# Block 0 of a two-layer kernel: second-layer steps placed between first-layer chunks, w_in and w_out rounded in turn

## Chip, cores, metric

The kernel runs on one core of one Trainium2 chip. The metric is device microseconds (us) of one execution, lower is better. PE is the matmul engine, with PEld its weight loads; DVE, ACT and POOL are the vector, scalar and GpSimd engines; SP only issues DMAs here. Each engine takes its instructions in order.

## What is computed

```python
w   = softmax(weight, axis=-1)               # 8 heads, 7 taps
y   = causal depthwise convolution of x      # x: (8, 4096, 192) float32
h   = y.reshape(32768, 192) @ w_in           # w_in: (192, 2048)
g   = h * clip(h + 3, 0, 6) / 6
out = g @ w_out                              # w_out: (2048, 192)
```

`w_in` and `w_out` arrive as 64-bit floats. The kernel rounds them to 32 bits itself, from their bits, once, while it works on its first tokens.

## The kernel before

The 32768 tokens are cut into 32 blocks of 1024, and a block into two groups of 512. In each block seven taps of convolution make y. **The first layer** makes g in 16 units. A unit holds one of 8 chunks c of d_ff for one group (128 columns of the lower half of d_ff, and 128 of the upper half for the other token group); unit n has c = n mod 8. It is 18 matmuls (three passes over high and low parts of weights and y, three thirds of the 192 channels, two row halves; `products`, L439) into the two PSUM banks of one of four slots. Then ACT takes the bounded part (`relu`, L302), DVE multiplies (`gate`, L306) and the slot is free again. Units 0 to 7 read y as the convolution leaves it (`y_own`). Units 8 to 15 read `y_other`, in which the two halves of the partitions are exchanged: SP issues these swaps as DMAs (L290, L291).

**The second layer** of blocks 1 to 31 is a recursive scheme with fewer products (`second_layer`, L535). Block 0 does it directly: 12 parts (2 token groups by 6 sets of 32 output columns), four to a bank, three banks; a bank sums 64 matmuls over 16 chunks of d_ff (`mm`, L317; one such matmul is two records in the trace). A bank is then transposed by DVE (L373) and stored by SP in four DMAs (L348).

**Rounding** works on units of its own, eight for `w_in` and eight for `w_out`, each 384 KB of 64-bit words. `load` is the DMA (L143 for w_in in two halves, L151 for w_out); `split` is two DVE instructions (L181, L185); `clamp` three on ACT (L193, L196, L199); `join` two on DVE (L202, L206) and one on POOL (L210). For w_in, `part` follows: L218 on ACT, L219 and L220 on POOL. The units are kept in the list `units` (L241): first all of w_in, then all of w_out. Four are loaded at the start, and each `join` loads the unit four further on. w_out's stages have four buffers.

**Block 0's order is written out by hand** (`tc.manual_schedule`). A part of the convolution is done by PE with diagonal weights (L739): all seven taps of the last third of the channels and taps 3 to 6 of third 1. First-layer work of units 0, 1 and 8 begins by thirds, as the thirds of y come (`thirds_of`, L759), in the order: units 0 thirds 2 and 0; unit 1 thirds 2 and 0; unit 0 third 1; unit 8 thirds 2 and 0; unit 1 third 1; unit 8 third 1. Then a loop (L813) takes the units in the order 0, 1, 8, 9, 2, 10, 3, 11 and so on; in every second step one rounding unit goes on (`join` in one step, `part`, `clamp` and `split` in the next). So w_in is rounded in the loop, and most of w_out after it. Then `out_direct` (L353) does the second layer bank by bank, and within a bank chunk by chunk. Its banks are in the first three free slots. On the other engines it is interleaved with `prepare` (block 1's seven taps, L845 on ACT and six of L847 on DVE, the high part on ACT, the low part L425 on DVE, and the load of block 2's x by POOL) and with `begin_block_two` (three sums of w_out on DVE, L237, sums on POOL, L507, and block 2's first three taps). Block 1's first layer follows on PE. Its first unit takes the first free slot.

Of the kernel before, what the change touches and what calls it, by code (L numbers as in the profile page):

```python
# [20 lines left out]
HIGH, LOW, FULL = range(3)  # L21
# [10 lines left out]
def kernel(  # L32
# [8 lines left out]
    nc = tc.nc  # L41
# [8 lines left out]
    G = 2  # L50
# [10 lines left out]
    NP = NC // 2  # L61
    DH = D // 2
    QS = 32
    NQ = DH // QS
# [97 lines left out]
    class Rounding:  # L162
# [10 lines left out]
        def load(self):  # L173
            self.st = self.load_words()

        def split(self, engine=nc.vector):
            high = self.st[:, :, 1]
            self.top = cnv.tile([P, WS], U32, name="top")
            self.scale = cnv.tile([P, WS], U32, name="scale")
            self.sig = cnv.tile([P, WS], F32, name="sig")  # L180
            engine.tensor_scalar(  # L181
                out=self.scale[:], in0=high, scalar1=0x7FF00000, scalar2=None,
                op0=ALU.bitwise_and,
            )
            engine.tensor_scalar(  # L185
                out=self.top[:], in0=high, scalar1=0xFFFFF, scalar2=0x100000,
                op0=ALU.bitwise_and, op1=ALU.bitwise_or,
            )
# [12 lines left out]
        def join(self):  # L201
            nc.vector.scalar_tensor_tensor(  # L202
                out=self.scale[:], in0=self.st[:, :, 1], scalar=0x80000000,
                in1=self.scale[:], op0=ALU.bitwise_and, op1=ALU.bitwise_or,
            )
            nc.vector.scalar_tensor_tensor(  # L206
                out=self.sig[:], in0=self.top[:], scalar=2.0**-20, in1=self.sig[:],
                op0=ALU.mult, op1=ALU.add,
            )
            nc.gpsimd.tensor_tensor(  # L210
                out=self.sig[:] if len(self.dst) > 1 else self.dst[0],
                in0=self.sig[:], in1=self.scale[:].bitcast(F32), op=ALU.mult,
            )
# [13 lines left out]
    def w_in_unit(j):  # L227
        dst = [w[:, j].rearrange("p s f -> p (s f)") for w in w_in_parts]
        return Rounding(lambda: load_w_in(j), dst)

    def w_out_unit(j):
        dst = w_out[:, j, B11 : B22 + 1].rearrange("p b d -> p (b d)")
        return Rounding(lambda: load_w_out(j), [dst])
# [4 lines left out]
                out=w_out[:, :, o], in0=w_out[:, :, x], in1=w_out[:, :, y], op=ALU.subtract  # L238
            )

    units = [w_in_unit(j) for j in range(NP)] + [w_out_unit(j) for j in range(NP)]  # L241
    AHEAD = 4
    for n in range(AHEAD):
        units[n].load()
# [59 lines left out]
    def gate(g_, h):  # L304

        nc.vector.scalar_tensor_tensor(  # L306
            out=g_, in0=g_, scalar=1.0, in1=h, op0=ALU.min, op1=ALU.mult
        )

    def dff_half(k):  # L310
        return g[:, :, k // G, k % G]

    def mm(bank, j, x, w, q, ps_, first, last, tokens=slice(0, N)):

        cols = slice(q * QS, (q + 1) * QS)
        return [
            lambda p=p: nc.tensor.matmul(  # L317
                out=bank[j * QS : (j + 1) * QS, tokens], lhsT=w_out[:, p, w, cols],
                rhs=x[:, p, tokens],
                start=(first and p == ps_[0]), stop=(last and p == ps_[-1]),  # L320
                tile_position=(0, j * QS),
            )
            for p in ps_
        ]

    def side_by_side(*streams):
        for mms in zip(*streams):
            for m in mms:
                m()

    every = range(NP)

# [6 lines left out]
    def next_xt():  # L339
        xts.append(xts.pop(0))  # L340
        return results[0][:, xts[-1]]
# [3 lines left out]
    def store_rows(i, k, q, xt, j, dma=nc.sync, tokens=slice(0, N)):  # L345

        t0 = i * TB + k * N
        dma.dma_start(  # L348
            out=out[t0 + tokens.start : t0 + tokens.stop, q * QS : (q + 1) * QS].rearrange("(t r) d -> r t d", r=QS),
            in_=xt[j * QS : (j + 1) * QS, tokens].rearrange("r (t d) -> r t d", d=QS),  # L350
        )

    def out_direct(i, work):  # L353

        parts = [(k, q) for k in range(G) for q in range(G * NQ)]
        for r in range(0, len(parts), 4):
            b = 2 * free_slots[r // 4]
            bank = psum[:, b]
            streams = []
            for j, (k, q) in enumerate(parts[r : r + 4]):  # L360
                streams.append([
                    m
                    for mms in zip(*(
                        mm(bank, j, dff_half(h * G + k), h * 2 + q // NQ, q % NQ, every,
                           h == 0, h == 1)
                        for h in range(2)
                    ))
                    for m in mms
                ])
            side_by_side(*streams)  # L370
            work[r // 4]()
            xt = next_xt()
            nc.vector.transpose(out=xt[:], in_=bank)  # L373
            for j, (k, q) in enumerate(parts[r : r + 4]):
                store_rows(i, k, q, xt, j)

    def g_sums(engine, which, slots, width):

# [42 lines left out]
    def high_of(out, x):  # L421
        nc.scalar.mul(r32(out), x, CUT)
# [6 lines left out]
    def swap_parts(thirds=slice(0, K3)):  # L429
        for n in range(2):  # L430
            swap(y_other[:, n, thirds], y_own[n][:, thirds])

    def products(n, slot, s, steps=range(3), begin=False, end=False):
        group, c = divmod(n, NP)
        for m_ in steps:
            wn, yn = PASSES[m_]
            for k in range(2):
                r = slice(k * D2, (k + 1) * D2)
                nc.tensor.matmul(  # L439
                    out=psum[:, 2 * slot + k], lhsT=r32(w_in_parts[wn][r, c, s]),  # L440
                    rhs=r32(y_other[r, yn, s] if group else y_own[yn][r, s]),
                    start=begin and m_ == 0, stop=end and m_ == 2, skip_group_check=True,
                )
# [269 lines left out]
        if n < len(units):  # L713
            units[n].load()

    def join(n, more=True):
        units[n].join()
        if more:
            load(n + AHEAD)

    def part(n):
        units[n].part()
# [1 line left out]
    with tc.manual_schedule():  # L724
# [7 lines left out]

        thirds = [slice(s, s + 1) for s in range(K3)]
        pe_third = K3 - 1
        pe_taps = 3
        x0 = x_tiles[0]

        def pe_tap(b, part, k, first):
# [20 lines left out]
        def thirds_of(n, which, end=False):  # L759
            if n not in early:  # L760
                early[n] = free_slots.pop(0)
            for s in which:
                products(n, early[n], s, begin=s == pe_third, end=end)

        def high_y(s, of):
            high_of(y_own[HIGH][:, thirds[s]], of)

        def low_y(s, of):
            low_of(y_own[LOW][:, thirds[s]], of, y_own[HIGH][:, thirds[s]], nc.vector)
            swap_parts(thirds[s])  # L770

        def all_of(s):
            return y[:, thirds[s]]
# [6 lines left out]
        clamp(0)  # L780
        for u in conv0[5 : per - 3]:
            u()
        join(0, more=False)
        split(1)
        high_y(pe_third, psum[:, b : b + 1])
        part(0)
        clamp(1)
        for u in conv0[per - 3 : per]:
            u()
        low_y(pe_third, psum[:, b : b + 1])  # L790
        high_y(0, all_of(0))
        low_y(0, all_of(0))
        load(AHEAD)
        thirds_of(0, (pe_third, 0))
        join(1)
        split(2)
        for u in conv0[per + 2 : per + 2 * pe_taps]:
            u()
        part(1)
        add(y[:, 1], psum[:, b1], y[:, 1])  # L800
        high_y(1, all_of(1))
        low_y(1, all_of(1))
        clamp(2)
        split(3)
        thirds_of(1, (pe_third, 0))
        thirds_of(0, (1,), True)
        thirds_of(NP, (pe_third, 0))
        thirds_of(1, (1,), True)
        thirds_of(NP, (1,), True)

        n = 2
        for at, k in enumerate([0, 1, NP, NP + 1] + [
            c + group * NP for c in range(2, NP) for group in range(2)  # L813
        ]):
            if at == 6:
                x_tiles[1] = load_x(1)
            if k in early:
                slot = early[k]
            else:
                slot = free_slots.pop(0)  # L820
                for m_ in range(3):
                    for s in range(K3):
                        products(k, slot, s, (m_,), s == 0, s == K3 - 1)
            to, both = places(k, slot)
            relu(to, both)
            if at % 2:
                part(n)
                clamp(n + 1)
            else:
                join(n)  # L830
            gate(to, both)
            free_slots.append(slot)
            if at % 2:
                split(n + 2)
                n += 1
        while n < len(units):
            join(n)
            clamp(n + 1)
            split(n + 2)
            n += 1  # L840
        start_pools.close()

        def conv_jobs(i):
# [32 lines left out]
            for job in conv[:3]:  # L876
                job()

        out_direct(0, [prepare, lambda: None, begin_block_two])
        swap_parts()  # L880
        w_sums(((T3, B22, B12),))
        last = ctx.enter_context(tc.tile_pool(name="last", bufs=1, reuse_waits="tile"))
# [52 lines left out]
```

## Time and profile before

| | |
|---|---|
| time of three runs | 2231.13, 2230.18, 2228.7 us; median 2230.18 |
| the profiled execution | 2230.25 us; span 2228.5 us |
| PE busy | 2212.9 us, 99% of the span |
| DVE, ACT, POOL busy | 81%, 42%, 37% |
| mean granted PE clock | 0.998 |
| first matmul of block 1's first layer | 104.61 us |
| PE idle in block 0's second layer, all for POOL's rounding of w_out | 6.3 us in 5 waits |

All times within the execution are counted from the start of its span. In a table by stretches of time, each engine has its busy us and, in brackets, its instructions; the columns behind POOL are the granted PE clock (1 is full), the mean busy share of the DMA engines, and GB/s. In a list by time, a row has its start, its length, engine, line, operation, output from input, shape, count, and in square brackets the idle time before it and what ended that. Instructions of one engine overlap a little, so a row may begin before the row above it has ended.

### The profile page before, as it was taken

What the parts mean: (1) busy time and instruction counts of PE and PEld (TensorE: products, weight loads), DVE (VectorE), ACT (ScalarE), POOL (GpSimd) and SP (SyncE); (2) the same over time, 40 slices, a digit from 0 to 9 for tenths busy, and PEclk for the clock granted to TensorE, in tenths of its full rate; (3) what the DMA queues carried; (4) which work ended last, traced back from release to release, by engine and by line L of the source; (5) the groups of instructions that cost most, each with busy time, mean ns of one, the idle gap of its engine ahead of it and who ended that gap; (6) DMA issues with size and microseconds to landing.
All of it is one profiled execution on the core that took longest, in us unless ns stands there. A gap on an engine that the chain in (4) does not pass through costs nothing.

```text
span 2228.5 us, 49336 instructions
## 1 busy us (share of the span) xinstructions
PE 2212.9 (99%) x21596; PEld 1537.8 (69%) x21596; DVE 1811.0 (81%) x1590; ACT 935.1 (42%) x1172; POOL 832.5 (37%) x706
## 2 busy tenths in 40 slices
PE   9899999999999999999999999999999999999999
PEld 6377776677766777666777667776677776677766
DVE  8778888888888888888888888788888888788866
ACT  7344433344433444334444334443344433344433
POOL 4344422344322444224443234442244422344322
PEclk9999999999999999999999999999999999999999
DMA  6233223332233332333322333323333223332232
GB/s 149 59 84 77 34 58 77 70 70 51 43 75 73 66 71 37 61 77 67 73 44 48 77 70 70 63 39 68 77 63 77 36 57 77 70 70 54 41 60 34
DMA packets 249095, 142.91 MB, mean 64 GB/s; under 512 B 207120, under 2 KB 212240, under 8 KB 248880
## 3 DMA queue, kind: packets, MB, share of 16 engines
q1 hardware_dynamic: 230392, 105.86, 23.5%
q0 software_dynamic: 17248, 33.64, 8.7%
q8 instruction: 169, 2.77, 0.5%
q10 hardware_dynamic: 1240, 0.27, 0.1%
q14 instruction: 46, 0.38, 0.1%
HBM read 31.72 MB, written 25.17 MB: 26 GB/s over the span
## 4 chain that ended last, share of the span: by engine, by line
PE 97%; ACT 1%; DVE 1%; POOL 0%; issue 0%; DMA 0%; DVEq 0%; ACTq 0%; SPq 0%; POOLq 0%
PE psum L535 49%; PE psum L439 46%; PE psum L317 1%; ACT g L302 1%; PE psum L739 0%; POOL w_out L210 0%; PE psum L747 0%; ACT scale L196 0%; DVE g L306 0%; ACT sig L199 0%; ACT sig L193 0%; DMA stage<-in_moe_w_out_dram 0%; ACT w_in L218 0%; DVE scale L202 0%; DVE sig L206 0%
## 5 line engine op out<-in xcount | busy, mean ns | idle before, releaser
L535 PE MATMUL psum<-g,w_out 128*32 128x512 f32 (+1 forms) x6712 | 967.4, 552 | 0.0
L302 ACT ACTIVATE g<-psum,half 128x1024 f32<-128x1024 f32 x512 | 571.6, 1118 | 495.4 <-PE psum L439 467.3
L306 DVE SCALAR_TENSOR_TENSOR g<-g,psum 128x1024 f32<-128x1024 f32 x512 | 618.3, 1218 | 198.1 <-ACT g L302 197.8
L498 POOL TENSOR_TENSOR s<-g 128x256 f32<-128x256 f32 x248 | 268.5, 1083 | 1251.0 <-DVE g L306 914.5
L535 PEld LDWEIGHTS psum<-g,w_out 128*32 128x32 f32 x6712 | 370.8, 110 | 246.9 <-issue 126.9
L439 PE MATMUL psum<-y,w_in 64*128 64x512 f32 x4608 | 535.8, 389 | 2.5 <-ACT w_in L218 1.8
L439 PE MATMUL psum<-y_other,w_in 64*128 64x512 f32 x4608 | 529.8, 387 | 0.0
L439 PEld LDWEIGHTS psum<-y,w_in 64*128 64x128 f32 x4608 | 430.1, 185 | 120.3 <-issue 26.0
L439 PEld LDWEIGHTS psum<-y_other,w_in 64*128 64x128 f32 x4608 | 432.7, 184 | 90.7
L535 PE MATMUL psum<-s,w_out 128*32 128x512 f32 (+1 forms) x3272 | 465.4, 570 | 0.0
L847 DVE SCALAR_TENSOR_TENSOR y<-x,c_sb,y 128x1536 f32<-128x1536 f32 x186 | 335.7, 1805 | 1.2
L387 POOL TENSOR_TENSOR s<-g 128x1024 f32<-128x1024 f32 x93 | 297.7, 3201 | 25.1 <-DVE g L306 25.1
L535 PE MATMUL psum<-g,w_s 128*32 128x256 f32 x1240 | 282.8, 379 | 0.0
L535 PEld LDWEIGHTS psum<-s,w_out 128*32 128x32 f32 x3272 | 153.7, 110 | 80.1 <-issue 48.4
L535 PEld LDWEIGHTS psum<-g,w_s 128*32 128x32 f32 x1240 | 136.4, 110 | 68.3
L387 DVE TENSOR_TENSOR s<-g 128x2048 f32<-128x2048 f32 (+1 forms) x93 | 177.1, 1931 | 1.1
L535 PE MATMUL psum<-s,w_s 128*32 128x256 f32 x744 | 170.7, 379 | 0.0
L498 DVE TENSOR_TENSOR g<-g 128x1024 f32<-128x1024 f32 x124 | 151.7, 1223 | 5.3
L387 DVE TENSOR_TENSOR g<-g 128x2048 f32<-128x2048 f32 x62 | 139.0, 2283 | 0.0
L407 DVE TENSOR_TENSOR p<-psum,p 32x256 f32<-32x256 f32 (+1 forms) x93 | 47.8, 514 | 96.3 <-PE psum L535 94.8
L407 DVE TENSOR_TENSOR results<-psum,results 32x256 f32<-32x256 f32 (+3 forms) x128 | 69.3, 541 | 51.2 <-issue 47.6
L532 ACT COPY psum<-psum 32x512 f32<-32x512 f32 x93 | 51.3, 551 | 135.4 <-PE psum L535 135.4
(88 smaller groups left out, 1094.2 us busy)
## 6 DMA issues: line engine op xcount, KB each, us to landing
y_other<-y SPq DMA_DIRECT2D x124, 384.0 KB, 5.0
g<-g POOLq DMA_DIRECT2D x62, 512.0 KB, 5.0
out_dram<-results SPq DMA_DIRECT2D x378, 64.0 KB, 2.0
x<-in_x_dram SPq DMA_DIRECT2D x53, 388.5 KB, 7.1
g<-in_moe_w_in_dram SPq DMA_DIRECT2D x16, 192.0 KB, 5.1
stage<-in_moe_w_out_dram SPq DMA_DIRECT2D x8, 384.0 KB, 7.8
x<-in_x_dram SPq DMA_DIRECT2D x7, 384.0 KB, 6.4
y_other<-y SPq DMA_DIRECT2D x12, 128.0 KB, 2.3
```

The lines of the kernel that those rows point to most:

```text
L302: nc.scalar.activation(r6, h, ACT.Relu, bias=half[:], scale=1.0 / 6.0)
L306: nc.vector.scalar_tensor_tensor(out=g_, in0=g_, scalar=1.0, in1=h, op0=ALU.min, op1=ALU.mult)
L317: lambda p=p: nc.tensor.matmul(out=bank[j * QS : (j + 1) * QS, tokens], lhsT=w_out[:, p, w, cols], rhs=x[:, p, tokens], start=(first and p ...
L387: engine.tensor_tensor(out=o[:, r], in0=a[:, r], in1=b[:, r], op=op)
L407: nc.vector.tensor_tensor(out=out, in0=x, in1=y, op=op)
L439: nc.tensor.matmul(out=psum[:, 2 * slot + k], lhsT=r32(w_in_parts[wn][r, c, s]), rhs=r32(y_other[r, yn, s] if group else y_own[yn][r, s]), ...
L498: engine.tensor_tensor(out=o, in0=p, in1=q, op=op)
L532: streams[3].append((t - 0.5, lambda: fn(*args, **kw)))
L535: nc.tensor.matmul(out=out, lhsT=w, rhs=x, start=start, stop=True, tile_position=(0, j * QS), skip_group_check=True,)
L847: jobs.append(lambda k=k: nc.vector.scalar_tensor_tensor(out=y[:], in0=x[:, :, k : k + N], scalar=c_sb[:, k : k + 1], in1=y[:], op0=ALU.mu ...
```

## The change

It concerns block 0 alone.

1. `units` alternates: w_in 0, w_in 1, then w_in 2, w_out 0, w_in 3, w_out 1, and so on to w_in 7, w_out 5; then w_out 6 and 7.
2. PE does one tap more of third 1 (2 to 6), DVE one less. The swaps are issued for each part as it is ready, the high one ahead of the low one. Rounding unit 1 is split after the low parts of thirds 2 and 0 and no longer ahead of them.
3. Loads 4 to 7 are issued together after the swaps of thirds 2 and 0, ahead of those of third 1; loads 8, 9, 10 and 12 after third 1's swaps; loads 11, 13, 14 and 15 in the loop.
4. The early units are 0 and 8: both thirds 2 and 0, then both third 1. Unit 1 is no longer early.
5. The loop takes the units by chunk: 0, 8, 1, 9, 2, 10, ... A rounding unit is joined in every step from the third on.
6. The slot of the third unit is not given back after its gate: its two banks hold the second layer's first two banks. After the sixth, eighth, ... sixteenth unit PE does 16 matmuls of the second layer, those of one chunk for these two banks (`direct_chunk`).
7. After the loop: `prepare`, chunks 6 and 7 of the two banks, their transposes and stores, the slot given back; then all eight chunks of the third bank, in the first free slot; `begin_block_two`; the third bank's transpose and stores.

```diff
-    units = [w_in_unit(j) for j in range(NP)] + [w_out_unit(j) for j in range(NP)]
+    units = [w_in_unit(0), w_in_unit(1)]
+    for j in range(2, NP):
+        units += [w_in_unit(j), w_out_unit(j - 2)]
+    units += [w_out_unit(j) for j in range(NP - 2, NP)]
...
-    def out_direct(i, work):
...
+    direct = [(k, q) for k in range(G) for q in range(G * NQ)]
+    direct = [direct[r : r + 4] for r in range(0, len(direct), 4)]
+
+    def direct_chunk(banks, p):
+
+        for h in range(2):
+            for r, bank in banks:
+                for j, (k, q) in enumerate(direct[r]):
+                    for m in mm(bank, j, dff_half(h * G + k), h * 2 + q // NQ, q % NQ,
+                                every[p : p + 1], h == 0 and p == 0, h == 1 and p == NP - 1):
+                        m()
+
+    def direct_out(i, r, bank):
+        xt = next_xt()
+        nc.vector.transpose(out=xt[:], in_=bank)
+        for j, (k, q) in enumerate(direct[r]):
+            store_rows(i, k, q, xt, j)
...
-        pe_taps = 3
+        pe_taps = 2
...
         def high_y(s, of):
             high_of(y_own[HIGH][:, thirds[s]], of)
+            swap(y_other[:, HIGH, thirds[s]], y_own[HIGH][:, thirds[s]])
 
         def low_y(s, of):
             low_of(y_own[LOW][:, thirds[s]], of, y_own[HIGH][:, thirds[s]], nc.vector)
-            swap_parts(thirds[s])
+            swap(y_other[:, LOW, thirds[s]], y_own[LOW][:, thirds[s]])
...
-        join(0, more=False)
-        split(1)
+        join(0)
         high_y(pe_third, psum[:, b : b + 1])
         part(0)
-        clamp(1)
         for u in conv0[per - 3 : per]:
             u()
         low_y(pe_third, psum[:, b : b + 1])
         high_y(0, all_of(0))
         low_y(0, all_of(0))
-        load(AHEAD)
+        for n in range(AHEAD, 2 * AHEAD):
+            load(n)
         thirds_of(0, (pe_third, 0))
-        join(1)
-        split(2)
+        thirds_of(NP, (pe_third, 0))
+        split(1)
+        clamp(1)
         for u in conv0[per + 2 : per + 2 * pe_taps]:
             u()
-        part(1)
         add(y[:, 1], psum[:, b1], y[:, 1])
         high_y(1, all_of(1))
+        join(1)
+        part(1)
         low_y(1, all_of(1))
+        for n in (8, 9, 10, 12):
+            load(n)
+        split(2)
         clamp(2)
         split(3)
-        thirds_of(1, (pe_third, 0))
         thirds_of(0, (1,), True)
-        thirds_of(NP, (pe_third, 0))
-        thirds_of(1, (1,), True)
         thirds_of(NP, (1,), True)
...
+        joins = {0: 2, **{n - 1: n for n in range(3, len(units))}}
+        loads = {3: 11, 5: 13, 7: 14, 9: 15}
...
+        for r in range(2 * NP):
+            c, group = divmod(r, 2)
+            k = c + group * NP
...
             relu(to, both)
+            n = joins.get(r)
+            if r - 1 in joins:
+                part(joins[r - 1])
+            if n is not None:
                 clamp(n + 1)
+                join(n)
+                if n in loads:
+                    load(loads[n])
+            gate(to, both)
+            if r == 2:
+                taken = slot
+                banks = [(h, psum[:, 2 * slot + h]) for h in range(2)]
+                x_tiles[1] = load_x(1)
             else:
+                free_slots.append(slot)
+            if n is not None:
                 split(n + 2)
+            if r >= 5 and r % 2:
+                direct_chunk(banks, (r - 5) // 2)
...
-        out_direct(0, [prepare, lambda: None, begin_block_two])
+        prepare()
+        for p in every[NP - 2 :]:
+            direct_chunk(banks, p)
+        for r, bank in banks:
+            direct_out(0, r, bank)
+        free_slots.append(taken)
+        third = 2, psum[:, 2 * free_slots[0]]
+        for p in every:
+            direct_chunk([third], p)
+        begin_block_two()
+        direct_out(0, *third)
```

More of the change, by code (lines that the diff above doesn't have):

```diff
@@ L320, in mm @@
                 start=(first and p == ps_[0]), stop=(last and p == ps_[-1]),
-                tile_position=(0, j * QS),
+                tile_position=(0, j * QS), skip_group_check=True,
             )
@@ L324, in mm @@
         ]
[L326 to L329, printed above, removed]
     every = range(NP)
@@ L351, in store_rows @@
         )
-    def out_direct(i, work):
[L355 to L375, printed above, removed]
+    direct = [(k, q) for k in range(G) for q in range(G * NQ)]
[12 more added lines that the diff above has]
+            store_rows(i, k, q, xt, j)
     def g_sums(engine, which, slots, width):
@@ L714, in load, with join @@
             units[n].load()
-    def join(n, more=True):
+    def join(n):
         units[n].join()
-        if more:
-            load(n + AHEAD)
     def part(n):
@@ L761, in thirds_of @@
                 early[n] = free_slots.pop(0)
-            for s in which:
-                products(n, early[n], s, begin=s == pe_third, end=end)
+            for m_ in range(3):
+                for s in which:
+                    products(
+                        n, early[n], s, (m_,), s == pe_third, end and s == which[-1]
+                    )
         def high_y(s, of):
             high_of(y_own[HIGH][:, thirds[s]], of)
+            swap(y_other[:, HIGH, thirds[s]], y_own[HIGH][:, thirds[s]])
         def low_y(s, of):
             low_of(y_own[LOW][:, thirds[s]], of, y_own[HIGH][:, thirds[s]], nc.vector)
-            swap_parts(thirds[s])
+            swap(y_other[:, LOW, thirds[s]], y_own[LOW][:, thirds[s]])
         def all_of(s):
@@ L792 @@
         low_y(0, all_of(0))
-        load(AHEAD)
+        for n in range(AHEAD, 2 * AHEAD):
+            load(n)
         thirds_of(0, (pe_third, 0))
-        join(1)
-        split(2)
+        thirds_of(NP, (pe_third, 0))
+        split(1)
+        clamp(1)
         for u in conv0[per + 2 : per + 2 * pe_taps]:
             u()
-        part(1)
         add(y[:, 1], psum[:, b1], y[:, 1])
         high_y(1, all_of(1))
+        join(1)
+        part(1)
         low_y(1, all_of(1))
+        for n in (8, 9, 10, 12):
+            load(n)
+        split(2)
         clamp(2)
         split(3)
-        thirds_of(1, (pe_third, 0))
         thirds_of(0, (1,), True)
-        thirds_of(NP, (pe_third, 0))
-        thirds_of(1, (1,), True)
         thirds_of(NP, (1,), True)
[L811 to L816, printed above, removed]
+        joins = {0: 2, **{n - 1: n for n in range(3, len(units))}}
+        loads = {3: 11, 5: 13, 7: 14, 9: 15}
+        taken = None
+        waiting = [1]
+        for r in range(2 * NP):
+            c, group = divmod(r, 2)
+            k = c + group * NP
             if k in early:
@@ L825 @@
             relu(to, both)
-            if at % 2:
-                part(n)
+            n = joins.get(r)
+            if r - 1 in joins:
+                part(joins[r - 1])
+            if n is not None:
                 clamp(n + 1)
-            else:
[L830 to L833, printed above, removed]
+                join(n)
[6 more added lines that the diff above has]
+                x_tiles[1] = load_x(1)
+            else:
+                free_slots.append(slot)
+            if n is not None:
                 split(n + 2)
[L835 to L840, printed above, removed]
+            if r >= 5 and r % 2:
+                direct_chunk(banks, (r - 5) // 2)
         start_pools.close()
```

## The prediction, made before the changed kernel was run

> **What bounds the kernel now.** I read the page first: busy shares and the chain of waits.
>
> ```profile
> PE 2212.9 (99%) x21596; PEld 1537.8 (69%) x21596; DVE 1811.0 (81%) x1590; ACT 935.1 (42%) x1172; POOL 832.5 (37%) x706
> ...
> PE 97%; ACT 1%; DVE 1%; POOL 0%; issue 0%; DMA 0%; DVEq 0%; ACTq 0%; SPq 0%; POOLq 0%
> ```
>
> PE is the bound, and blocks 1 to 31 are left as they were. So the time moves with one moment, at which PE begins block 1 (call it X; 104.61 us before), and with any clock lost after it. Next, PE by time in block 0's second layer (start, length, row):
>
> ```profile
> 53.77 2.21 PE L439 MATMUL psum<-y_other,w_in 64*128 64x512 f32 x18
> 55.91 1.92 PE L317 MATMUL psum<-g,w_out 128*32 128x512 f32 x16
> 58.88 1.92 PE L317 MATMUL psum<-g,w_out 128*32 128x512 f32 x16 [1.05 <-POOL w_out L210]
> 62.72 1.92 PE L317 MATMUL psum<-g,w_out 128*32 128x512 f32 x16 [1.92 <-POOL w_out L210]
> 66.24 3.64 PE L317 MATMUL psum<-g,w_out 128*32 128x512 f32 x32 [1.59 <-POOL w_out L210]
> 71.00 3.64 PE L317 MATMUL psum<-g,w_out 128*32 128x512 f32 x32 [1.12 <-POOL w_out L210]
> 75.29 29.39 PE L317 MATMUL psum<-g,w_out 128*32 128x512 f32 x272 [0.65 <-POOL w_out L210]
> 104.61 0.50 PE L439 MATMUL psum<-y,w_in 64*128 64x512 f32 x2
> ```
>
> 384 records at 0.107 (29.39 / 272 = 0.108) are 41.1 of the 48.7 us from 55.91 to 104.61. The other 7.6, five waits for rounded w_out with their tails, is all that the change can win here. The start, by stretches of 2 us (PE, PEld, DVE, ACT, POOL, then clock, DMA share, GB/s):
>
> ```profile
> 18.00:20.00 2.00, 0.23 (x4) 0.00 (x0) 2.00 (x4) 0.51 (x1) 1.52 (x2) 1.00 0.94 207
> 20.00:22.00 2.00, 1.27 (x6) 0.86 (x8) 2.00 (x4) 0.01 (x1) 1.12 (x2) 0.74 0.82 182
> 22.00:24.00 2.00, 1.97 (x12) 1.06 (x10) 1.20 (x3) 0.92 (x2) 0.00 (x0) 0.50 0.95 267
> 24.00:26.00 2.00, 2.00 (x10) 1.53 (x12) 1.96 (x5) 1.94 (x4) 0.00 (x0) 0.50 1.08 219
> 26.00:28.00 2.00, 2.00 (x12) 1.52 (x10) 1.27 (x2) 0.57 (x1) 1.51 (x2) 0.55 0.87 189
> ```
>
> PE stands idle from 18.2 to 20.1; then the granted clock is 0.50 until 27.8 (0.55 over the last 2 us), though PE works again from 21.23: 6.6 us at half speed, 3.3 lost. And the DMA engines are full (0.82 to 1.08) at 207, 182, 267, 219, 189: 213 GB/s on average. At 31.2 us four of the 16 units are through PE. Last, what DVE does before block 1, and ACT's first tap of block 2:
>
> ```profile
> 72.58 11.69 DVE L847 SCALAR_TENSOR_TENSOR y<-x,c_sb,y 128x1536 f32<-128x1536 f32 x6
> 85.82 1.76 DVE L425 TENSOR_TENSOR y<-y,y 128x1536 fp32r<-128x1536 f32 x1 [1.55 <-ACT y L422]
> 87.50 0.71 DVE L373 STREAM_TRANSPOSE results<-psum 128x512 f32<-128x512 f32 x1
> 91.02 0.72 DVE L373 STREAM_TRANSPOSE results<-psum 128x512 f32<-128x512 f32 x1 [2.81 <-PE psum L317]
> 91.66 3.04 DVE L237 TENSOR_TENSOR w_out<-w_out 128x768 f32<-128x768 f32 x3
> 94.62 3.94 DVE L847 SCALAR_TENSOR_TENSOR y<-x,c_sb,y 128x1536 f32<-128x1536 f32 x2
> 104.75 0.72 DVE L373 STREAM_TRANSPOSE results<-psum 128x512 f32<-128x512 f32 x1 [6.19 <-PE psum L317]
> ```
> ```profile
> 91.61 1.58 ACT L845 ACTIVATE y<-x,c_sb 128x1536 f32<-128x1536 f32 x1 [5.83 <-DMA x<-in_x_dram]
> ```
>
> DVE is there 6.19 us ahead of the third bank: this slack is what the change spends.
>
> **The change, part by part.**
>
> *The waits for w_out go (up to -7.6).* Two loop steps cost ACT two relus (1.12), two clamps (0.60 + 0.62 + 0.57) and a part (0.52), 6.3 us; DVE two gates (1.22), two splits (0.35 + 0.35) and joins (0.55 + 0.55), 6.0; POOL 3.6 (L210 1.03 twice, L219 0.51, L220 1.03). PE now has 36 first-layer matmuls (2.04 a unit) and 16 second-layer ones (32 records, 3.43): 7.5. So rounding is hidden under PE from the sixth unit on; from the third to the fifth PE has three slots to run ahead in. If DVE and POOL held each other up fully, it would be 6.0 - 2.4 of gates + 3.6 = 7.2, still under 7.5; that cover is thin.
>
> *The swaps of third 1 stand behind twice the loads.* Before, SP issued 768 KB of loads at 20.47 and then the four swaps, which took 2.9 to 3.2 us each and had landed at 28.5 (last issue 25.6). In the changed order the first eight swaps begin again at 13.88 and, their data being early enough without split 1 and clamp 1 ahead of them, follow each other at 0.6: until 18.7. Six loads of 1536 KB follow until 22.5, the last swap at 24.3. From 15.2 on (landing starts some 1.3 after issue) the DMA engines must move 1536 KB of swaps (1024 and the last 512) and 768 of w_in at 213 GB/s, 11.1 us, and 768 KB of w_out at the 253 GB/s of 28 to 36 us, 3.1: they end at 29.4. The same sum for before gives 27.9 where 28.5 was measured. The swap that waits for nothing in front of it would land at 24.3 + 2.9 = 27.2. I take 29.4, the row of a full queue being the nearer one. Behind unit 8's matmuls, which wait for it, stands every later matmul: unit 1 was early before, and is not now. With two last matmuls PE goes on at 29.6, two units through.
>
> *Third 1's tap (+0.86 PE, -0.95 DVE) and the earlier low parts* cost nothing: the swaps above hide them; without that cover 0.9.
>
> *From there to the end of the 16th unit, T:* 14 units x 2.04 = 28.6, five chunks x 3.43 = 17.2, ten more changes between the two kinds of matmul. Such a change shows in the rows at 55.91 and 104.61 as 0.1 beyond the usual spacing: 1.0. The clock drops in the idle stretch from 21.5 to 28; bounds 0 and the 3.3 shown, and as the low stretch here begins while PE waits, I take three quarters, 2.5. T = 29.6 + 28.6 + 17.2 + 1.0 + 2.5 = 78.9. Four units are through at 29.6 + 4.1 + 2.5 = 36.2, at 31.2 before: the start loses 5 of the 7.6. Hidden are the other moved DMAs: block 1's x, issued at 29.6 before, is issued some 5 later and needed at T; block 1's swaps follow the third bank's four stores, some 3 after X, and are needed eight units, 16.3, after X.
>
> [...]
>
> *The third bank: a new wait.* PE needs three chunks more of two banks (10.3), then 64 matmuls (13.7): done at T + 24.1 = 103.0, 1.6 before the old X. But the third bank lies in the first free slot, and block 1's first unit takes that slot: PE must wait for the transpose, which stands on DVE behind `prepare` and `begin_block_two`. That chain starts with the 16th gate: relu 0.36 after T, and gate over 2.7 after T (107.01 to 109.38 in block 1, 2.37); ACT's first tap, 1.57, ends at T + 3.0. From 72.58 the rows give: low part done at 87.58 (+15.0), two transposes to 88.9, sums 3.0 to 91.9, ACT's tap of block 2 until 93.2 (its x arrives no earlier), two taps 3.9 to 97.1, transpose to 97.8: +25.2. So X = T + 28.2 = 107.1. PE waits 4.1 us.
>
> *After that wait the clock drops again.* 1.84 us of idleness did it at 20 us; waits of up to 1.92 in the stretch 56 to 75 did not, at a clock of 1.00. 4.1 is well above both; bounds 0 and 3.3, I take 2.5.
>
> [...]
>
> **Sum**: X 107.1 - 104.6 = +2.5, clock +2.5: +5.0. The profiled execution took 2230.25 (span 2228.5), 0.07 above the median of the runs: **2235.2**.
>
> **The rivals.**
>
> 1. *Forecast*, both waits and both clock losses: 2235.2, own range 2233 to 2238. Chance 0.52; four fifths of it above 2234.6.
> 2. *Only one clock loss* or smaller ones (the stretch is shown once only, and where it ends may shift): 2232.7, 0.20.
> 3. *Not slower: the swaps don't queue.* If they pass between the loads and land at 27.2, PE resumes at 27.4; decisive is whether the landing is below 27. With the clock kept T = 74.2, X = 102.4: -2.2, 2228. For it: SP's swaps took only 2.3 us at 17 to 20 us. Against: stages issued together at 31 took 9. Chance 0.10. If besides the third bank's transpose came in time (x of block 2 4 us earlier), X would be T + 24.2: -6.4, 2224. Chance 0.08.
> 4. *Rounding sets the pace after all*, DVE and POOL locking each other out (POOL's L210 took up to 2.50 beside DVE's taps, against 1.03), or dearer changes of matmul kind: 0.5 us a chunk more, 2238 to 2241. Chance 0.10.
>
> That the change wouldn't do what it says is excluded for PE's order, which is written by hand.
>
> A difference of 0.2% (4.5 us) is about what a measurement of this kernel can tell from none. Slower by more: 0.42 of the first and 0.10 of the fourth, 0.52; within: 0.10 + 0.20 + 0.10 = 0.40; faster: 0.08. Range 2228 to 2240: it takes in the third rival's time and most of the fourth's.
>
> **What would show it.** PE in the changed profile: idle from about 21.5 to 28, ended by DMA y_other; clock near 0.5 at 25 to 33; L317's successors in blocks of 32 records between pairs of units, without waits for POOL; the 16th unit ending at 79; second layer ending at 103; then idleness of 4 us, ended by DVE's transpose, and a low clock after it; X near 107. Wrong it would be if PE resumed before 27, if block 1 began right behind the third bank, or if waits for POOL remained in the loop.

## The result, and the profile after

The changed kernel takes **2235.02 us** (median of 10 runs, 2233.26 to 2237.44), the kernel before 2229.93 (10 runs, 2228.7 to 2231.13): ratio 1.0024, 95% interval 1.0014 to 1.0034. It is slower by about 5 us. The profiled execution of the changed kernel took 2237.14 us (span 2235.0), 2.1 above its median; so its trace shows +6.5 of span, and each step below is held against that.

The page of the changed kernel, busy shares and the chain that ended last:

```profile
PE 2216.5 (99%) x21598; PEld 1543.1 (69%) x21598; DVE 1811.7 (81%) x1588; ACT 936.0 (42%) x1172; POOL 829.0 (37%) x706
...
PE 97%; DVE 1%; DMA 1%; SPq 0%; ACT 0%; issue 0%; POOL 0%; DVEq 0%; ACTq 0%; POOLq 0%
```

PE is the bound as before. New in the chain is DMA at 1%, in place of ACT. PE by time in block 0 (start, length, row):

```profile
21.04 0.85 PE L433 MATMUL psum<-y,w_in 64*128 64x512 f32 x6
29.20 2.16 PE L433 MATMUL psum<-y_other,w_in 64*128 64x512 f32 x6 [7.32 <-DMA y_other<-y]
31.16 4.04 PE L433 MATMUL psum<-y,w_in 64*128 64x512 f32 x18
...
41.54 3.64 PE L322 MATMUL psum<-g,w_out 128*32 128x512 f32 x32
...
80.95 24.24 PE L322 MATMUL psum<-g,w_out 128*32 128x512 f32 x224
108.23 17.11 PE L433 MATMUL psum<-y,w_in 64*128 64x512 f32 x124 [3.04 <-DVE results L367]
```

(The last row stops at the view's end, 125 us.) All of PE's waits for POOL's rounding of w_out are gone. Two others have come: 7.32 us for third 1's swaps, and 3.04 for the transpose of the third bank; a short one, 0.80 at 19.37, is for the earlier swaps. At the start, PE before waited for w_in's second rounding unit:

```profile
20.07 0.50 PE L439 MATMUL psum<-y,w_in 64*128 64x512 f32 x2 [1.83 <-ACT w_in L218]
```

That wait is gone too, since unit 1 is no longer early. X, the first matmul of block 1, is 108.23 (104.61 before): +3.62. The remaining 2.9 of the 6.5 lie behind X. The same stretches by windows of 2 us (PE, PEld, DVE, ACT, POOL, then granted clock, DMA share, GB/s):

```profile
24.00:26.00 2.00, 0.00 (x0) 0.00 (x0) 1.64 (x3) 1.41 (x3) 1.09 (x2) 0.84 0.86 212
28.00:30.00 2.00, 0.80 (x4) 0.50 (x4) 0.00 (x0) 0.00 (x0) 0.00 (x0) 0.50 1.10 233
34.00:36.00 2.00, 2.00 (x14) 1.52 (x14) 0.93 (x2) 0.75 (x1) 1.04 (x2) 0.60 0.77 149
...
106.00:108.00 2.00, 0.00 (x0) 0.00 (x0) 2.00 (x2) 0.00 (x0) 0.00 (x0) 0.82 0.00 0
112.00:114.00 2.00, 2.00 (x13) 1.67 (x12) 0.38 (x1) 1.11 (x1) 0.00 (x0) 0.50 1.00 197
114.00:116.00 2.00, 2.00 (x20) 1.76 (x18) 0.85 (x1) 0.62 (x1) 0.00 (x0) 0.97 0.94 250
```

Behind each wait PE works on at half clock: at the start until about 35.6, at the end until about 114.1. The clock steps between 1 and 0.50: in windows of 0.2 us it is 0.94 over 25.2 to 25.4 and 0.50 over 25.4 to 25.6, 0.50 over 35.4 to 35.6 and 0.96 over 35.6 to 35.8, 0.50 over 113.9 to 114.1 and 1.00 over 114.2 to 114.4. The end lies 5.9 us after X, so 2.9 are lost, which closes the sum. What DVE does meanwhile:

```profile
83.68 11.09 DVE L849 SCALAR_TENSOR_TENSOR y<-x,c_sb,y 128x1536 f32<-128x1536 f32 x6 [0.24 <-ACT y L847]
...
99.23 3.21 DVE L237 TENSOR_TENSOR w_out<-w_out 128x768 f32<-128x768 f32 x3
103.79 3.67 DVE L849 SCALAR_TENSOR_TENSOR y<-x,c_sb,y 128x1536 f32<-128x1536 f32 x2 [1.35 <-ACT y L847]
107.38 0.71 DVE L367 STREAM_TRANSPOSE results<-psum 128x512 f32<-128x512 f32 x1
```

The third bank was complete at 105.2 (80.95 + 24.24), but DVE reaches its transpose only at 107.38, behind taps and sums that belong to later blocks; before, DVE stood idle 6.19 us ahead of that transpose.

**Where the won time went.** Before, four units were through at 31.2; now the fifth begins at 37.36: 6.2 later. The waits for w_out are 7.6 less. The ten changes between the two kinds of matmul cost 1.9 (worked out below). The new wait at the end is 3.0. Sum: 6.2 - 7.6 + 1.9 + 3.0 = +3.5, where X moved by 3.62.

### The profile page after: what moved, and what is told of

It reads as the page before. It is cut to its first block, busy times and chain, and to the rows that moved or that the text cites. A ratio compares the mean times of both kernels' runs of the same rounds, so it can differ in the third digit from the quotient of the medians.

```text
span 2235.0 us, 49342 instructions
## 1 busy us (share of the span) xinstructions
PE 2216.5 (99%) x21598; PEld 1543.1 (69%) x21598; DVE 1811.7 (81%) x1588; ACT 936.0 (42%) x1172; POOL 829.0 (37%) x706
## 4 chain that ended last, share of the span: by engine, by line
PE 97%; DVE 1%; DMA 1%; SPq 0%; ACT 0%; issue 0%; POOL 0%; DVEq 0%; ACTq 0%; POOLq 0%
PE psum L529 49%; PE psum L433 47%; PE psum L322 1%; DVE y L849 1%; DMA x<-in_x_dram 0%; DMA y_other<-y 0%; SPq L143 0%; ACT y L847 0%; DVE y L284 0%; SPq L295 0%; SPq L105 0%; SPq L296 0%; SPq L151 0%; DVE results L401 0%; SPq L94 0%
## 5 line engine op out<-in xcount | busy, mean ns | idle before, releaser
L401 DVE TENSOR_TENSOR p<-psum,p 32x256 f32<-32x256 f32 (+1 forms) x93 | 47.7, 513 | 96.5 <-PE psum L529 95.1
```

The source lines that it names most:

```text
L401: nc.vector.tensor_tensor(out=out, in0=x, in1=y, op=op)
```

## The experiments

Theory: both losses come from the two waits and the clock behind them. The wait at the start is there because third 1's four swaps stand behind six loads in SP's queue; the one at the end because block 1's first unit takes the third bank's slot. Rivals: the alternating rounding sets the pace, or the changes between the kinds of matmul are dear; and, of the wait at the start, that the swaps would come late without the loads too. Every diff is against the changed kernel; a ratio is to the kernel before on the same chip (median 2229.86 for the first four kernels, 2229.59 for the others). Eleven runs each; five of the kernel with both cures.

The readings of the traces, in us; run 7, whose units stand alone, is read in its own place. "Units" is the time from the third unit's first matmul to the end of the 16th unit; "rest" is the difference of the span from before's less that of X, which is what was lost behind X:

| kernel | PE released by the swaps | units | wait at the end | X | span against before | rest |
|---|---|---|---|---|---|---|
| the change | 29.20 | 49.8 | 3.04 | 108.23 | +6.5 | 2.9 |
| another slot | 30.31 | 49.7 | none | 105.90 | +1.3 | 0.0 |
| swaps first | 23.50 | 47.65 | 3.06 | 98.79 | -4.2 | 1.6 |
| both | 23.32 | 47.7 | none | 95.48 | -9.0 | 0.1 |
| half the loads | 26.01 | 49.7 | 2.95 | 104.68 | +0.1 | 0.0 |
| end filled | 28.58 | 49.35 | filled | 107.16 | +2.4 | -0.1 |
| start filled | 31.47 | 48.3 | 2.99 | 108.76 | +5.9 | 1.7 |
| both filled | 30.03 | 47.6 | filled | 106.16 | +1.5 | 0.0 |

**1. Another slot for the third bank.** Block 1's third unit takes it, not its first.

```diff
-        third = 2, psum[:, 2 * free_slots[0]]
+        third = 2, psum[:, 2 * free_slots[2]]
```

> The changed kernel, with the third bank in the third free slot instead of the first. Two waits (my theory: the time is lost where PE waits for the swaps of third 1 and where block 1's first unit waits for the third bank's transpose, each with a lowered clock behind it): PE goes from the third bank's last matmul (105.1) straight into block 1; the idle 3.0 us and the 2.9 us of lowered clock behind it go; 2235.0 falls to 2229.5 (2228.5 to 2231). The pace (rival: the time is lost in alternating two kinds of matmul and in rounding that sets the pace, and block 1 waits for DVE's chain whatever slot it takes): PE then waits in its second or third unit instead, 2234 to 2236.

Measured: 2230.45 (2229.95 to 2231.96), ratio 1.0004 [0.9995, 1.0012]. PE by time:

```profile
81.73 24.24 PE L322 MATMUL psum<-g,w_out 128*32 128x512 f32 x224
105.90 16.61 PE L433 MATMUL psum<-y,w_in 64*128 64x512 f32 x144
```

Block 1 begins right behind the third bank, eight units (144 matmuls) take 16.61 and the clock stays at 1.00. The slot alone, with the clock behind it, was worth 4.6 us of the median.

**2. The swaps first.** All eight loads after third 1's swaps.

```diff
-        for n in range(AHEAD, 2 * AHEAD):
-            load(n)
...
-        for n in (8, 9, 10, 12):
+        for n in (4, 5, 6, 7, 8, 9, 10, 12):
             load(n)
```

> The changed kernel, with loads 4 to 7 issued after the swaps of third 1. Two waits: the last swap lands near 23.5 instead of 30.5, PE's wait falls from 7.3 us to below 2.5, the 16th unit ends near 74 instead of 80.9, and all behind it, the wait for the third bank's transpose included, comes 7 us earlier: 2228 (2225.5 to 2229.5). The pace: with PE early, ACT's 6.3 us in two steps and the later loads of w_in hold the units up, and less than 4 us is won: 2231 to 2234.

Measured: 2226.23 (2224.53 to 2226.83), ratio 0.9981 [0.9972, 0.999]. PE by time, and the DMA issues between 19 and 31 us (output from input, queue, operation, count, KB of one, median us from issue to landing):

```profile
23.50 0.50 PE L433 MATMUL psum<-y_other,w_in 64*128 64x512 f32 x2 [0.62 <-DMA y_other<-y]
23.84 2.24 PE L433 MATMUL psum<-y,w_in 64*128 64x512 f32 x18
...
98.79 18.17 PE L433 MATMUL psum<-y,w_in 64*128 64x512 f32 x144 [3.06 <-DVE results L367]
```
```profile
y_other<-y SPq DMA_DIRECT2D x5, 128.0 KB, 2.3
```

The wait at the start shrinks from 7.32 to 0.62 with no clock lost there (1.00 from 18 to 38); the wait at the end stays at 3 us. (The fifth swap in this row belongs to an earlier third.) The first load is issued at 21.72 and not at 18.94, and still no loop step waits for weights: the rounding has that much slack. The order of the loads was worth 8.8 us of the median.

**3. Both of them.**

```diff
-        for n in range(AHEAD, 2 * AHEAD):
-            load(n)
...
-        for n in (8, 9, 10, 12):
+        for n in (4, 5, 6, 7, 8, 9, 10, 12):
             load(n)
...
-        third = 2, psum[:, 2 * free_slots[0]]
+        third = 2, psum[:, 2 * free_slots[2]]
```

> Both edits: the third bank in the third free slot, and loads 4 to 7 after the swaps of third 1. Two waits: the gains add, as they lie one behind the other on PE: 7 + 5.5, so 2222.5 (2221 to 2225), faster than the kernel before by 0.3%; block 1 begins near 98. The pace: 2230 or more.

Measured: 2221.61 (2221.57 to 2221.96), ratio 0.9963 [0.9951, 0.9976]. This version beats both kernels, and the two cures add up: 13.4 us for both, 4.6 + 8.8 for one and the other. From the third unit on, PE has no wait left in block 0:

```profile
23.65 2.25 PE L433 MATMUL psum<-y,w_in 64*128 64x512 f32 x18
...
71.31 24.24 PE L322 MATMUL psum<-g,w_out 128*32 128x512 f32 x224
95.48 16.61 PE L433 MATMUL psum<-y,w_in 64*128 64x512 f32 x144
```

This excludes the pace of the rounding as a cause. It also prices the changes of matmul kind: 14 units x 2.04 + 5 chunks x 3.43 = 45.7 of the 47.7 between 23.65 and 71.31, so some 1.9 for ten changes, 0.19 each. X is 9.1 earlier than before: 3.4 at the start (four units through at 27.8, not 31.2), 7.6 for the waits, less 1.9.

**4. Half the loads ahead** of third 1's swaps: 768 KB, all w_in, where the change has 1536.

```diff
-        for n in range(AHEAD, 2 * AHEAD):
+        for n in (4, 6):
             load(n)
...
-        for n in (8, 9, 10, 12):
+        for n in (5, 7, 8, 9, 10, 12):
             load(n)
```

> The changed kernel, with only w_in's two of the four loads (768 KB, as much as before the change) issued ahead of the swaps of third 1, and w_out's two behind them. Two waits, with the swaps queued behind the bytes in front of them: half the bytes gone is 3 us, the last swap lands at 27.4 instead of 30.5 and the time is 2232 (2230.5 to 2233.5). If the swaps are late for another reason (their issue by SP, or late data), landing moves by the 1.2 us that SP saves, and the time is 2233.5 to 2235.

Measured: 2230.51 (2230.09 to 2231.23), ratio 1.0004 [0.9995, 1.0013], at the lower edge of what queueing by bytes gave. The issues of third 1's swaps, first in the change (22 to 31 us), then here (19 to 31 us):

```profile
y_other<-y SPq DMA_DIRECT2D x4, 128.0 KB, 5.9
```
```profile
y_other<-y SPq DMA_DIRECT2D x4, 128.0 KB, 3.6
```

From issue to landing: 2.3 us with no load ahead, 3.6 behind 768 KB, 5.9 behind 1536 KB; PE goes on at 23.50, 26.01, 29.20. The swaps wait for the loads in front of them. Whether their bytes or their number decides is not separated: 1536 KB are six DMAs, 768 KB four. The end of this trace brought a surprise: a wait of the same length, with no loss of clock. PE, and the windows around it:

```profile
104.68 16.63 PE L433 MATMUL psum<-y,w_in 64*128 64x512 f32 x144 [2.95 <-DVE results L367]
```
```profile
102.00:104.00 2.00, 0.00 (x0) 0.00 (x0) 1.97 (x3) 0.00 (x0) 0.00 (x0) 1.00 0.00 0
104.00:106.00 2.00, 1.32 (x12) 1.29 (x14) 2.00 (x3) 0.00 (x0) 0.00 (x0) 1.00 0.27 42
```

**5. The wait at the end filled** with 26 first-layer matmuls into the two banks that have just been stored, 0.12 us each. They add work, and nothing reads what they write.

```diff
+        def idle_pairs(slot, count):
+            for _ in range(count):
+                for k in range(2):
+                    r = slice(k * D2, (k + 1) * D2)
+                    nc.tensor.matmul(out=psum[:, 2 * slot + k], lhsT=r32(w_in_parts[HIGH][r, 0, 0]), rhs=r32(y_own[HIGH][r, 0]), ...)
...
+        idle_pairs(taken, 13)
         begin_block_two()
```

> The changed kernel, with 26 first-layer matmuls (13 pairs, 2.95 us) added on PE while it waits for the third bank's transpose; they write two banks that nobody reads before they are overwritten, so the result is the same. If the lowered clock behind that wait comes from PE's idleness, the clock stays at 1.0 past 108, block 1 begins at 108.2 as before, and the median falls by what the drop costs in a typical run: 2233.3 (2232 to 2234.5). In the traces so far a wait of 3.0 us cost 2.9, 1.6 and nothing, so the spread of 4 us between runs should shrink too. If the drop has another cause, or is already paid elsewhere: 2235.

Measured: 2233.56 (2232.6 to 2235.54), ratio 1.0019 [1.001, 1.0028].

```profile
104.08 3.24 PE L764 MATMUL psum<-y,w_in 64*128 64x512 f32 x26
107.16 16.51 PE L433 MATMUL psum<-y,w_in 64*128 64x512 f32 x144
```

From the 16th unit's end (79.91) to X it takes 27.25 us as in the change (27.28), but with PE busy, and the clock stays full behind it (1.00 from 102 to 116): eight units in 16.51. One trace would not be enough, as run 4 kept its clock behind an idle wait; but over the runs the median falls by 1.5 us (2235.02 less 2233.56), and the distance between the extremes from 4.2 to 2.9. So it is the idleness that costs the clock. The size is rough: the kernel before was 0.3 faster in this measurement, which leaves 1.1 to 1.5 us, half or less of the 2.9 of the one profiled execution.

**6. The wait at the start filled**, with 60 such matmuls.

```diff
         thirds_of(0, (1,), True)
+        idle_pairs(free_slots[0], 30)
         thirds_of(NP, (1,), True)
```

> The changed kernel, with 60 first-layer matmuls (30 pairs, 6.8 us) added on PE while it waits for the swaps of third 1, into two banks of a slot that is not in use yet; the result is the same. Clock from idleness: it stays at 1.0 at 29, the third and fourth unit take 2.04 us instead of 3.8 and 2.4, the 16th unit ends 2 to 2.5 us earlier: 2232.6 (2231.5 to 2233.8). If the matmuls run into the landing of the swaps (they end at 28.7, and swaps landed at 29.2 and 30.3), up to 0.5 more. If clock doesn't matter, 2235.

Measured: 2234.19 (2232.89 to 2236.99), ratio 1.0023 [1.0014, 1.0032]. Missed. The profiled execution (2236.46 us, 2.3 above the median) shows one way in which the filling fails:

```profile
21.98 6.97 PE L764 MATMUL psum<-y,w_in 64*128 64x512 f32 x60
31.47 1.93 PE L433 MATMUL psum<-y_other,w_in 64*128 64x512 f32 x6 [2.52 <-DMA y_other<-y]
```

In this execution the swaps released PE 2.3 us later than in the change's, at 31.47 and not at 29.20, and the 60 matmuls had ended at 28.95. PE was idle 2.52 us after all, and the clock fell (0.80 over 30 to 32, 0.50 over 32 to 34). By itself this run settles nothing on the clock at the start.

**7. The chunks after the loop**: both cures, but all 16-matmul steps of the first two banks behind the 16th unit, as the kernel before has its second layer.

```diff
-            if r >= 5 and r % 2:
-                direct_chunk(banks, (r - 5) // 2)
...
-        for p in every[NP - 2 :]:
+        for p in every:
             direct_chunk(banks, p)
```

> The kernel with both edits (swaps of third 1 ahead of loads 4 to 7, third bank in the third free slot; 2221.6), but with all chunks of the first two banks after the loop: what the interleaving is worth by itself, the rounding staying in turn. Without second-layer work between the units, ACT's 6.3 us in two steps set the pace: 14 units from 23.7 at 3.1 are 43.4, the 16th ends near 68, then 41.1 of second layer: block 1 near 109 instead of 95.5, 2235 (2231 to 2237). If the rounding in turn is what pays, and not the place of the chunks, the time stays below 2225.

Measured: 2231.43 (2231.15 to 2232.03), ratio 1.0008 [0.9999, 1.0017], nearer to the kernel before than expected: the 16th unit ends at 63.96, not 68. PE now waits in the loop, for the parts of w_in:

```profile
34.25 1.04 PE L433 MATMUL psum<-y,w_in 64*128 64x512 f32 x6 [2.09 <-ACT w_in L218]
...
63.96 41.41 PE L322 MATMUL psum<-g,w_out 128*32 128x512 f32 x384
105.30 16.61 PE L433 MATMUL psum<-y,w_in 64*128 64x512 f32 x144
```

Rounding in turn alone gains nothing, for w_in then comes too slowly. The interleaved steps are what covers it, and they are worth 9.8 us (2231.43 less 2221.61). In the trace 5.9 us of that are PE's waits in the loop, and some 2.9 are slower matmuls behind the first of them: twelve take 2.72 us from 35.87 on and the next eighteen 3.57, where eighteen take 2.04 elsewhere. So the first twelve run at half speed. That the clock was at 0.50 there is an estimate from these rows; no window shows it for this run.

**8. Both waits filled**, 5 and 6 together.

```diff
+        idle_pairs(free_slots[0], 30)
         thirds_of(NP, (1,), True)
...
+        idle_pairs(taken, 13)
         begin_block_two()
```

> Both sets of added matmuls: the changed kernel with its two waits as they are, and no lowered clock behind them. The difference to the kernel before is then what the waits alone cost, by my sums +1 to +1.5: 2231 (2230 to 2232), and the spread between runs is below 1.5 us. The rest of the 5.1 is the clock.

Measured: 2232.85 (2231.92 to 2236.49), ratio 1.0018 [1.0009, 1.0026]. Median and spread missed: 4.6 us between the extremes where under 1.5 was expected. In the profiled execution (2232.1 us) the remaining idle time at the start is short, and the clock is 1.00 from 22 to 38 and from 102 to 116:

```profile
30.03 0.73 PE L433 MATMUL psum<-y_other,w_in 64*128 64x512 f32 x4 [1.32 <-DMA y_other<-y]
```

Here the units take 47.6, as where nothing was lost, and 49.8 in the change: the clock at the start costs 2.1 behind the third unit's begin. X moves by 1.55 only, and the span with it: that is what the two waits alone cost, all gains deducted. The spread that is left fits the landing of the swaps, which released PE between 28.58 and 31.47 in the five traces with this order of loads; in other runs the 60 matmuls may not have reached it. That last step is argued, not shown.

## Why the prediction was right, step by step

The mechanism is the one forecast, and so is the size, 2235.2 against 2235.02. Part of that closeness is chance: in the profiled execution the terms come to +6.5 and not +5.0, while over the runs the kernel is 5.1 slower.

- **The waits for w_out go: right**, all of them, and no wait for POOL or ACT is left in the loop. "All that the change can win" was wrong. With both cures X comes 9.1 earlier, not at most 7.6: the change also rearranges the loads, and before's own loss at the start (waits of 1.83 and 0.66 us for w_in's second rounding unit, and 3.3 of clock) could be won as well, as unit 1 is no longer early. The prediction priced that clock loss and did not count it as something to gain.
- **The swaps queue behind the loads: right.** Landing at 29.4 was forecast; the last swap, issued at 24.63, comes to 30.5 by the median landing of 5.9. Runs 2 and 4 show the cause. The third rival falls.
- **The third unit at 29.6: 1.6 too early** (31.16). Of this 1.0 is the clock: at half speed from 29.20 to 35.6 it loses 3.2 in all, 1.0 before the third unit and the rest after. The term of 2.5 was mis-sized; the upper bound, 3.3, was nearly it.
- **49.3 from there to T: 49.8.** The units and chunks were right. Ten changes cost 1.9, not 1.0: the two rows of before, at 0.1, gave half of it. The remaining clock took 2.1. The price is 0.19 us each, a third of one second-layer matmul (0.59 us, the mean of L322). No run shows what the 0.19 us are made of.
- **T + 28.2 for the DVE chain: 27.3.** The shape was right, down to the taps of block 2 ahead of the transpose. Six taps took 11.09 and not 11.69, two 3.67 and not 3.94. With the third bank done at 105.2, the wait is 3.04, where 4.1 was forecast.
- **The clock behind that wait, 2.5**: 2.9 in the profiled execution, 1.1 to 1.5 of the median (run 5). That the clock would fall was right; the row it was taken from was misread. The 0.74 over 20 to 22 puts the fall before the change at 21.0 (0.92 over 20.8 to 21.0, 0.50 over 21.0 to 21.2), 2.7 us after PE had stopped at 18.2 and with 0.5 us of work in between, so not after 1.84 us of idleness alone. The second rival, only one clock loss, can happen: run 4's trace has a wait of 2.95 at full clock.
- **Rounding as the pace, the fourth rival: fallen** (runs 1 to 3). Its other half, dearer changes of matmul kind, came true by 0.9 us in all, some 0.2 a chunk, where the rival asked for 0.5.

The sum of the errors: 2.0 late at T (80.95 against 78.9), 0.9 less in DVE's chain, 0.4 more clock: 1.5 more than the +5.0 forecast, which is the +6.5 of the trace.

**Open**: what the clock at the start costs over many runs, which run 6 was to isolate; and why the release of PE by the same swaps varies by 2.9 us (28.58 to 31.47) between the five traces with this order of loads. The change and run 1 issue the last of them at 24.63 and 24.69 and release PE at 29.20 and 30.31.

## What to carry to other kernels

Issue the small transfer that the bound engine needs next ahead of the large loads on its queue, and price what stands in front of it: here 1536 KB ahead of four swaps cost 8.8 us, the clock behind the wait included, and the loads themselves lost nothing by going later. When a buffer is put to a second use, look up who takes it next and where the instruction that frees it stands in its engine's queue; one index was worth 4.6 us. A change that removes one wait is to be read with the waits that it brings and the clock behind them: the interleaving here is worth 9.8 us, and two orders around it took away 13.4.

## What the runs showed of the hardware

The clock after a short idleness is not a fixed price. Waits of 3.04, 3.06, 2.99 and 2.95 us at the same place lost 2.9, 1.6, 1.7 and 0 us. The windows show where these sizes come from. Here are those of run 2 (first two) and run 6:

```profile
98.00:100.00 2.00, 1.21 (x6) 1.11 (x8) 2.00 (x4) 0.00 (x0) 0.00 (x0) 0.68 0.19 30
102.00:104.00 2.00, 2.00 (x20) 1.72 (x18) 0.15 (x1) 1.12 (x1) 0.00 (x0) 0.97 0.91 179
```
```profile
108.00:110.00 2.00, 1.24 (x10) 1.21 (x12) 2.00 (x3) 0.00 (x0) 0.00 (x0) 0.93 0.20 31
112.00:114.00 2.00, 2.00 (x16) 1.97 (x14) 0.61 (x1) 1.12 (x1) 0.00 (x0) 0.72 0.94 190
```

With a clock that steps between 1 and 0.50, as the windows of 0.2 us show it in the change, the low stretch is at 98.7 to 102.1 in run 2 and at 109.7 to 113.1 in run 6, 3.4 us each. In the change the stretches are 25.4 to 35.6 and 107.3 to 114.1, 10.2 and 6.8 us; before the change, 21.0 to 27.8, 6.8 us. The longest, 25.38 to 35.62 by the windows of 0.2 us, is three times 3.41, and all are one, two or three times that. The two falls in the change lie 81.9 us apart, 24 times 3.41; those in run 6, at 31.2 and 109.7, lie 23 times 3.41 apart. So the clock's changes in these traces fit moments 3.41 us apart, and the same wait meets them differently in each execution. That is why the fall at the end came 2.1 us after PE stopped in the change, 3.0 in run 2, and 3.9 in run 6, where PE had already gone on.

What must happen between two such moments is less sharp. In the 3.41 us ahead of a fall PE was busy for 0 us (the change, start), 1.3 (the change, end) and 1.5 (run 5, start). In run 4, where the spacing puts a moment at 103.7, it was busy for 1.4 and the clock stayed.

Spread goes with such waits: the change runs over 4.2 us (ten runs), the version without either wait over 0.4 (five runs).
